# Thresholded attention and a feed-forward on one core: scores of pairs 2 and 3 computed twice, thresholds subtracted by the matrix engine, and a new order of the work

## The chip, the core and the metric

The kernel runs on one core of a Trainium2 chip. The core has a matrix engine (TensorE, PE in the profile; its weight loads are PEld), a vector engine (VectorE, DVE), a scalar engine for activation functions (ScalarE, ACT), a general engine (GpSimd, POOL) and an engine that here only issues transfers (SyncE, SP). Each runs its own list of instructions; they wait for each other through semaphores. Data lie in the main memory (DRAM), in the on-chip memory of 128 partitions, or in PSUM, the memory that PE writes its sums to. The metric is the device time of one execution in microseconds (us), as the median of several runs.

## The reference

Attention over 8 batches with 8 heads of 576 positions and 64 features, in which only scores near the maximum of their row count; then a feed-forward of two matrix products over the 4608 positions with 512 features:

```python
scores = scale * np.matmul(q, k.transpose(0, 1, 3, 2))
thresh = np.max(scores, axis=-1, keepdims=True) - tau
scores = np.where(scores >= thresh, scores, -1000000000.0)
scores = scores - np.max(scores, axis=-1, keepdims=True)
attn = np.exp(scores)
attn = attn / (np.sum(attn, axis=-1, keepdims=True) + 1e-09)
out = np.matmul(attn, v)
# x: the heads side by side, (4608, 512)
h = x @ w_in                              # 512 -> 2048
g = h * (1.0 / (1.0 + np.exp(-1.702 * h)))
return g @ w_out                          # 2048 -> 512
```

tau is 0.02. The weights arrive as 64-bit floats.

## The kernel before

**Pairs of heads.** The 64 heads are worked on as 32 pairs, n = 0 to 31, four to a batch. For a pair, q and k are loaded (`load_qk`, four DMAs each on SP's queue) and transposed by DVE (`prep`, L477). PE computes the scores with the keys in the partitions, one key tile j of 64 keys at a time, nine tiles in all (`scores`, L493: four matmuls of 64x288 for two heads and two halves of the queries). ACT copies each from PSUM (`keep`, L510). DVE takes the maxima over groups of keys (`in_groups`, L516, with a transpose in the instruction), then over tiles (`over_tiles`, L525) and over the halves of the keys (`over_halves`, L536 to L547), where the gap tau/scale is also subtracted. The thresholds, one for each query, must then be spread over all partitions. For pairs in `BY_DMA` they go through a row in DRAM: `turn_rows` (L553), `row_out` (L566) and `row_in` (L575), on SP's queue. Pair 2 alone uses a DVE transpose instead (`spread_max`, L557). Then, for double key tiles t, DVE subtracts the thresholds from the scores (`sub`, L580), ACT drives what is negative to a huge negative number (`mask`, L586) and takes the exponential (`exps`, L590), and PE multiplies by the values (`values`, L601).

**Denominators.** For pairs 0 to 4 PE sums the exponentials with a matrix of ones (`sums_by_pe`, L601) and DVE reads the sums (`one_row`, L632). For the others DVE sums in groups. For pairs 5 to 7 the sums are folded and spread by DVE (`one_group`, L643 to L647, `spread_sums`, L684 to L686); from pair 8 on they go through a row in DRAM (`turn_sums`, `sums_out`, `sums_in`). `place_x` (L703) multiplies the values by the reciprocals and places the pair in the input of the feed-forward.

**Feed-forward.** It runs in blocks of 256 positions. The first two blocks go together and need pairs 0 to 3 (`mm1_0`, L758, then ACT's tanh, L727, and DVE's `gelu_0`, L764, then `mm2`, L740). The third block needs pairs 4 to 7, and so on. From the third block on (first products at L718) the second product takes seven block products in place of eight, and the last four blocks do so for the first one too (L823, L909). The weights come in 32 pieces of 1 MB on POOL's queue (`load_w`, L428 and L429). DVE and ACT turn each into 32-bit floats (L439, L453, L457, L465 on DVE, L447 on ACT). The places where the pieces land are free again only after a piece before them is done.

**The order.** Nothing is scheduled by hand. Each step is recorded as a task with an engine, a cost, a rank, the tasks that it comes after, and the buffers that it takes and gives back. `run_in_order` then plays the tasks through with these costs, and writes each engine's list in the order in which they start. A rank is the number of the pair plus a bias by the step's name, from the tables `EARLY` (pairs 0 to 3), `SECOND` (4 to 7), `LATER` and `CV` (weights). The lists are fixed afterwards: an instruction waits behind the one in front of it on its engine, whatever the chip does.

**Buffers that matter.** `psA` has three PSUM buffers for scores and values, `psM` two for denominators and the feed-forward. A single row buffer serves the thresholds of one pair at a time. The value tau is loaded on POOL's queue at the start; `tau_terms` on DVE needs it.

The lines that choose the pairs:

```python
BY_PE = 5
BY_DMA = (0, 1, *range(3, NP))
SUMS_BY_DMA = range(8, NP)
```

Of the kernel before, what the change touches and what calls it, by code (L numbers as in the profile page):

```python
# [19 lines left out]
P = 128  # L20
# [10 lines left out]
def kernel(  # L31
# [84 lines left out]
    stop = const.tile([P, 1], FP32, name="stop")  # L116
    shift = const.tile([P, 1], FP32, name="shift")
# [9 lines left out]
    for x in ("raw0", "raw1", "qkT0", "qkT1", "mb"):  # L127
# [6 lines left out]
        "exps": -11.47,  # L134
        "in_groups": 5.75,
        "keep": 10.66,
        "load_qk": -0.27,
        "load_v": 4.86,
        "mask": -2.66,
        "one_group": -15.86,  # L140
        "one_row": 12.67,
        "over_halves": -7.01,
        "over_tiles": -4.01,
        "place_x": -17.11,
        "prep": -11.73,
        "row_in": 20.49,
        "row_out": 4.47,
        "scores_run": 12.45,
        "spread_max": -1.73,
        "spread_sums": 7.14,  # L150
        "sub": 9.27,
        "sums_by_pe": 0.27,
        "sums_in": -9.39,
        "sums_out": 2.13,
        "turn_rows": -12.55,
        "turn_sums": -0.41,
        "values": 14.64,
        "w_sum": 4.11,
        "x_sum": -14.1,
    }  # L160
    SECOND = {
        "exps": -7.29,
        "in_groups": 20.95,
        "keep": 16.67,
        "load_qk": -8.88,
        "load_v": 5.53,
        "mask": 2.36,
        "one_group": 2.55,
        "one_row": -2.71,
        "over_halves": -12.07,  # L170
        "over_tiles": 2.86,
        "place_x": -20.26,
        "prep": 3.49,
        "row_in": -19.42,
        "row_out": -24.08,
        "scores_run": -7.99,
        "spread_max": -3.11,
        "spread_sums": -2.29,
        "sub": 14.98,
        "sums_by_pe": 35.93,  # L180
        "sums_in": 7.43,
        "sums_out": 4.05,
        "turn_rows": -3.84,
        "turn_sums": 4.03,
        "values": 11.79,
        "w_sum": -10.45,
        "x_sum": -10.98,
    }
    LATER = {
        "exps": 2.01,  # L190
        "in_groups": 10.37,
        "keep": -0.02,
        "load_qk": -6.6,
        "load_v": 3.77,
        "mask": 14.79,
        "one_group": 4.78,
        "one_row": -14.98,
        "over_halves": 1.09,
        "over_tiles": -6.27,
        "place_x": -0.34,  # L200
        "prep": 2.34,
        "row_in": 4.02,
        "row_out": 2.64,
        "scores_run": -11.25,
        "spread_max": -9.44,
        "spread_sums": -6.73,
        "sub": 2.14,
        "sums_by_pe": 1.46,
        "sums_in": 3.78,
        "sums_out": 2.16,  # L210
        "turn_rows": 12.26,
        "turn_sums": 0.29,
        "values": -10.38,
        "w_sum": 6.61,
        "x_sum": 6.02,
    }
    CV = {
        "cv_end": -8.05,
        "cv_ex": 2.22,
        "cv_frac": -11.72,  # L220
        "cv_power": -4.72,
        "load_w": -7.79,
    }

    LAG = {"PE": 0.26, "DVE": 0.18, "ACT": 0.22, "POOL": 0.18}

    QUARTERS = ("scores", "scores_run", "values", "sums_by_pe")
# [12 lines left out]
    FIRST, LAST = -9.0, 1000.0  # L240
    need, follows = {}, {}

    def run_in_order():
# [12 lines left out]
        while events:  # L256
# [18 lines left out]
            for engine, queue in ready.items():  # L275
                if engine in busy:
                    continue
                for rank, i in sorted(queue):
# [25 lines left out]
    JOINT = 7  # L304

# [183 lines left out]
    def scores(n, j):  # L489
# [8 lines left out]
        if j == NK - 1:  # L498
            del mats[n, 0], mats[n, 1]
# [32 lines left out]
    def over_halves(n):  # L532
        r = stats[n, ALU.max]
        o = work.tile([P, QB], FP32, name="fold", tag="fold", bufs=1)
        for x in (1, 3) if n in BY_DMA else range(4):
            nc.vector.tensor_scalar(  # L536
                out=o[ts(x ^ 1, 32)], in0=r[ts(x, 32)], scalar1=gap[ts(x, 32)], scalar2=None,
                op0=ALU.subtract,
            )
        if n in BY_DMA:  # L540
# [10 lines left out]
    def turn_rows(n):  # L551

        nc.vector.transpose(out=flat[1], in_=flat[0])  # L553

# [23 lines left out]
    def sub(n, t):  # L578
        s = sT[n, t].rearrange("p u h s -> p u (h s)")
        nc.vector.tensor_tensor(  # L580
# [26 lines left out]
    def values(n, tiles):  # L607
# [4 lines left out]
        if n < NPAIR:  # L612
# [763 lines left out]
```

## Time and profile before

| | us |
|---|---|
| median of 3 runs | 1318.74 (1318.22 to 1318.92) |
| the profiled execution, its time | 1317.94 |
| its span, first to last instruction | 1316.2 |
| pair 3 placed (start of L703) | 114.40 |
| last weight piece ready (L465) | 215.3 |
| pair 7 placed (start of L703) | 276.40 |
| first product of the third block (L718) | 280.23 |

The costliest groups on the three busy engines are these (line, engine, operation, output and inputs, count; then busy time and the mean of one in ns; then the idle time ahead of them and what ended it).

```profile
L516 DVE TRANSPOSE_TENSOR_REDUCE part<-arena 128x36 f32<-128x1152 f32 (+1 forms) x295 | 357.5, 1235 | 41.9 <-ACT arena L510 32.4
L718 PE MATMUL hps<-xT,w_in 128*128 128x256 f32 x1536 | 337.2, 380 | 0.5 <-DVE arena L730 0.4
L510 ACT COPY arena<-ps 128x576 f32<-128x576 f32 x288 | 170.7, 647 | 115.3 <-PE ps L493 111.9
L580 DVE TENSOR_TENSOR arena<-arena 128x1152 f32<-128x1152 f32 (+1 forms) x158 | 201.1, 1313 | 20.5 <-DMA arena<-row 20.5
L493 PE MATMUL ps<-arena 64*64 64x288 f32 x2304 | 174.7, 420 | 22.9 <-DVE arena L477 15.3
```

A matmul of 32-bit floats appears as two records, so the 1152 score matmuls of 32 pairs are 2304 records; [...]the mean of 420 ns is not the time between two of them. DVE's subtraction is one of its large groups. PE's idle time ahead of the scores waits mostly for DVE's transposes in the start-up.

### The profile page before, as it was taken

The numbers are of one execution on the slowest core, as the hardware profiler recorded it, in microseconds if no ns is written. First come the engines' busy times: TensorE is split into PE (matmuls) and PEld (weight loads), VectorE is DVE, ScalarE is ACT, GpSimd is POOL, SyncE is SP. The second block draws the span as 40 slices with busy tenths as digits, with TensorE's granted clock in tenths as the row PEclk, the third lists the DMA queues.
The fourth block names the chain that finished last, engine by engine and source line by source line (L and its number), as shares of the span: only waits on it lengthen the run. The fifth ranks groups of instructions, "written<-read, shape, count | busy, mean of one in ns | idle before, by whom it ended". The sixth has DMA issues, their size and how long they took to land. (4 is left out here: it accounts for less than half of the span.)

```text
span 1316.2 us, 22807 instructions
## 1 busy us (share of the span) xinstructions
PE 1260.9 (96%) x9128; PEld 975.6 (74%) x9128; DVE 1006.1 (76%) x1610; ACT 646.6 (49%) x830; POOL 249.0 (19%) x291
## 2 busy tenths in 40 slices
PE   5669999999999999999999999999999999999998
PEld 2346864457887777777778888777777778888887
DVE  7989999898888887788777877777888863652642
ACT  4876666576554555555554555454556540210210
POOL 1201211012031211213021303030212117120120
PEclk8879999999999999999999999999999999999999
DMA  8976766545323223212213222323122110000000
GB/s 152 293 189 207 230 207 149 112 77 100 85 55 71 55 55 71 51 50 54 58 42 72 55 71 55 71 55 71 36 55 54 36 46 8 9 1 25 8 0 32
DMA packets 258819, 102.88 MB, mean 78 GB/s; under 512 B 233754, under 2 KB 243994, under 8 KB 258714
## 3 DMA queue, kind: packets, MB, share of 16 engines
q1 hardware_dynamic: 244986, 63.40, 22.4%
q0 software_dynamic: 11360, 37.74, 9.3%
q8 instruction: 71, 1.16, 0.4%
q10 hardware_dynamic: 2368, 0.30, 0.2%
q14 instruction: 34, 0.28, 0.1%
HBM read 87.51 MB, written 9.69 MB: 74 GB/s over the span
## 5 line engine op out<-in xcount | busy, mean ns | idle before, releaser
L516 DVE TRANSPOSE_TENSOR_REDUCE part<-arena 128x36 f32<-128x1152 f32 (+1 forms) x295 | 357.5, 1235 | 41.9 <-ACT arena L510 32.4
L718 PE MATMUL hps<-xT,w_in 128*128 128x256 f32 x1536 | 337.2, 380 | 0.5 <-DVE arena L730 0.4
L718 PEld LDWEIGHTS hps<-xT,w_in 128*128 128x128 f32 x1536 | 290.7, 190 | 45.9 <-issue 5.7
L586 ACT ACTIVATE arena<-arena 128x1152 f32<-128x1152 f32 (+1 forms) x160 | 169.4, 1059 | 144.0 <-DVE arena L580 143.8
L510 ACT COPY arena<-ps 128x576 f32<-128x576 f32 x288 | 170.7, 647 | 115.3 <-PE ps L493 111.9
L580 DVE TENSOR_TENSOR arena<-arena 128x1152 f32<-128x1152 f32 (+1 forms) x158 | 201.1, 1313 | 20.5 <-DMA arena<-row 20.5
L909 PE MATMUL ops<-w_out,arena 128*128 128x256 f32 x896 | 202.4, 380 | 1.8 <-DVE arena L730 1.8
L590 ACT ACTIVATE arena<-arena,shift,scl 128x1152 f32<-128x1152 f32 (+1 forms) x160 | 200.3, 1252 | 4.1
L493 PE MATMUL ps<-arena 64*64 64x288 f32 x2304 | 174.7, 420 | 22.9 <-DVE arena L477 15.3
L909 PEld LDWEIGHTS ops<-w_out,arena 128*128 128x128 f32 x896 | 169.3, 190 | 28.7 <-DVE arena L730 3.1
L875 POOL TENSOR_TENSOR arena<-arena 128x256 f32<-128x256 f32 x56 | 49.7, 888 | 647.1 <-DVE arena L730 543.9
L601 PE MATMUL pv<-arena 64*64 64x288 f32 x2176 | 159.7, 408 | 0.0
L727 ACT ACTIVATE th<-hps 128x512 f32<-128x512 f32 x112 | 66.0, 589 | 186.0 <-PE hps L718 171.8
L909 PE MATMUL ops<-arena 128*128 128x256 f32 x672 | 150.7, 380 | 0.7 <-DVE osb L931 0.7
L493 PEld LDWEIGHTS ps<-arena 64*64 64x64 f32 x2304 | 84.0, 137 | 90.8 <-ACT arena L510 30.4
L909 PEld LDWEIGHTS ops<-arena 128*128 128x128 f32 x672 | 127.1, 190 | 20.4 <-issue 2.2
L601 PEld LDWEIGHTS pv<-arena 64*64 64x64 f32 x2176 | 82.1, 134 | 54.1 <-issue 10.0
L931 DVE SCALAR_TENSOR_TENSOR osb<-ops,osb 128x256 f32<-128x256 f32 x98 | 39.3, 413 | 97.9 <-PE ops L909 90.6
L730 DVE SCALAR_TENSOR_TENSOR arena<-th,hps 128x512 f32<-128x512 f32 x96 | 64.2, 669 | 46.7 <-ACT th L727 46.4
L740 PE MATMUL ops<-w_out,arena 128*128 128x512 f32 x128 | 57.2, 600 | 3.2 <-DVE w_out L465 2.2
L758 PE MATMUL hps<-xT,w_in 128*128 128x256 f32 x256 | 56.4, 381 | 0.0
L888 POOL TENSOR_TENSOR arena<-arena 128x512 f32<-128x512 f32 x28 | 35.6, 1272 | 108.3 <-PE ops L909 108.3
(115 smaller groups left out, 1044.7 us busy)
## 6 DMA issues: line engine op xcount, KB each, us to landing
arena<-in_v_dram SPq DMA_DIRECT2D x128, 144.0 KB
arena<-in_q_dram SPq DMA_DIRECT2D x128, 72.0 KB
out_dram<-osb SPq DMA_DIRECT2D x36, 256.0 KB
arena<-in_k_dram SPq DMA_DIRECT2D x124, 72.0 KB
arena<-row SPq DMA_DIRECT2D x62, 144.0 KB
arena<-row_s SPq DMA_DIRECT2D x48, 144.0 KB
w_out<-in_moe_w_in_dram POOLq DMA_DIRECT2D x12, 512.0 KB, 9.5
arena<-in_moe_w_out_dram POOLq DMA_DIRECT2D x12, 512.0 KB, 6.3
```

The costliest lines, as they stand in the source:

```text
L493: nc.tensor.matmul(ps[ts(c, KT), h, 0:SH], lhsT=mats[n, 1][ts(h, D), ts(j, KT)], rhs=mats[n, 0][ts(h, D), ts(c, SH)], start=True, stop=True,)
L510: nc.scalar.copy(out=sT[n, t][:, u], in_=pss.pop((n, j))[:, :, 0:SH])
L516: nc.vector.tensor_reduce(out=stats[n, op][:, t * 2 * QB : min(2 * t + 2, NK) * QB], in_=sT[n, t].rearrange("p u h (g d) -> p (u h g) d", ...
L580: nc.vector.tensor_tensor(out=s, in0=s, in1=mbs[n].unsqueeze(1).to_broadcast(list(s.shape)), op=ALU.subtract)
L586: nc.scalar.activation(out=s, in_=s, func=AF.Prelu, alpha=STEEP)
L590: nc.scalar.activation(out=s, in_=s, func=AF.Exp, scale=scl, bias=shift)
L601: nc.tensor.matmul(o[c][ts(h, D), 0:SH], lhsT=left(j, h)[ts(c, KT)], rhs=sT[n, t][ts(c, KT), u, h, :], start=(j == 0), stop=(j == NK - 1),)
L718: nc.tensor.matmul(hidden[j][:, ts(f, BLK)], lhsT=w_in[:, c, ds((f * HF + j) * P, P)], rhs=xTs[blk][:, c, :], start=(c == 0), stop=(c == N ...
L727: nc.scalar.activation(out=ths[j], in_=hidden[j], func=AF.Tanh, scale=GELU_SCALE / 2)
L730: nc.vector.scalar_tensor_tensor(out=g[:, :, j, :], in0=two(ths.pop(j)), scalar=1.0, in1=two(hidden.pop(j)), op0=ALU.add, op1=ALU.mult,)
L740: nc.tensor.matmul(acc[i], lhsT=g0[:, j, ts(i, P)], rhs=w_out[:, j, :], start=(j == 0), stop=(j == NFC - 1),)
L909: nc.tensor.matmul(banks[blk][k][:, ts(o, HM)], lhsT=left[:, j, :], rhs=right[:, j, :], start=(j == 0), stop=(j == HF - 1),)
```

## The change

It has four parts.

1. **Pairs 2 and 3 (`TWICE`).** DVE no longer subtracts. The thresholds are laid out on DVE as a matrix that has, in each partition, only the queries of one group (`row_blocks`: a small transpose and a product with `own_row`, a matrix of ones and zeros). When the maxima are known, PE computes each score tile again (`again`), and adds to the same PSUM sum the product of this matrix with `minus`, which holds -1 and 0. ACT masks straight out of PSUM (`mask_one`, nine for a pair) into the place where the copied scores lay. Pair 3 no longer sends its thresholds through DRAM, and pair 2 no longer uses `spread_max`. `minus` and `own_row` are set up once on POOL, in front of tau's load.
2. **Sums of pairs 5 to 7** go through a row in DRAM, as those of pairs 8 and later do.
3. **The planner** has two more servers, DMS and DMW, for transfers from SP's and POOL's queues. A load is now a task for the issue and a task for the transfer, with a cost, one at a time on each server and in the order of arrival. Some costs of tasks are new. `BY_POOL`, which would move subtractions to POOL, is empty.
4. **All ranks** (`EARLY`, `SECOND`, `LATER`, `CV`, `W_RANK`) are new.

```diff
+    minus = const.tile([P, 2, KT], FP32, name="minus")
+    own_row = const.tile([P, QB // 2], FP32, name="own_row")
...
+    MOVERS = ("DMS", "DMW")
+    def transfer(by, time, a, give=(), lag=1.7):
+        return task(by, time, FIRST, moved, after=[a], give=give, lag=lag)
...
-                for rank, i in sorted(queue):
+                for rank, i in queue if engine in MOVERS else sorted(queue):
...
+    TWICE = (2, 3)
+    BY_POOL = {}
...
+        if n in TWICE:
+            for x, y in ((0, 0), (1, 2), (2, 1), (3, 3)):
+                nc.vector.scalar_tensor_tensor(
+                    out=flat[0][ts(y, 32), 0:QB], in0=r[ts(x, 32)], scalar=gap[ts(x, 32)],
+                    in1=o[ts(x, 32)], op0=ALU.subtract, op1=ALU.max,
+                )
+            return
...
+    def row_blocks(n):
+        nc.vector.transpose(out=flat[1], in_=flat[0])
+        mb = home(n, "mb")[:, 0:SH]
+        nc.vector.tensor_tensor(
+            out=mb.rearrange("p (g i) -> p g i", i=32),
+            in0=flat[1].unsqueeze(1).to_broadcast([P, QB // 2, 32]),
+            in1=own_row.unsqueeze(2).to_broadcast([P, QB // 2, 32]), op=ALU.mult,
+        )
+        mbs[n] = mb
+
+    def again(n, j):
+        ps = psA.tile([P, 2, 512], FP32, name="ps", tag="ps")
+        for first in (True, False):
+            for h in range(2):
+                for c in range(2):
+                    if first:
+                        left = mats[n, 1][ts(h, D), ts(j, KT)]
+                        right = mats[n, 0][ts(h, D), ts(c, SH)]
+                    else:
+                        left, right = minus[ts(h, D), c, :], mbs[n][ts(h, D), :]
+                    nc.tensor.matmul(
+                        ps[ts(c, KT), h, 0:SH], lhsT=left, rhs=right, start=first, stop=not first,
+                    )
...
+    def mask_one(n, j):
+        nc.scalar.activation(
+            out=sT[n, j // 2][:, j % 2], in_=pss.pop((n, j))[:, :, 0:SH], func=AF.Prelu, alpha=STEEP
+        )
...
+    nc.gpsimd.memset(minus, 0.0)
+    nc.gpsimd.memset(own_row, 0.0)
+    for x in range(4):
+        nc.gpsimd.memset(minus[ts(x, 32), x % 2, :], -1.0)
+        nc.gpsimd.affine_select(
+            out=own_row[ts(x, 32)], in_=own_row[ts(x, 32)], compare_op=ALU.not_equal, fill=1.0,
+            base=-(QB // 2) * (x // 2), pattern=[[-1, QB // 2]], channel_multiplier=1,
+        )
     nc.gpsimd.dma_start(
         out=tau_b, in_=bass.AP(tensor=tau.tensor, offset=tau.offset, ap=[[0, P], [1, 1]])
     )
...
-    BY_PE = 5
-    BY_DMA = (0, 1, *range(3, NP))
-    SUMS_BY_DMA = range(8, NP)
+    SUMS_BY_PE = (0, 1, 2, 3, 4)
+    BY_DMA = (0, 1, *range(4, NP))
+    SUMS_BY_DMA = range(5, NP)
...
-        a = task("POOL", 1.1, rank, load_w, i, after=w_loads[-1:], take=place, lag=9.0)
+        a = task("POOL", 1.1, rank, load_w, i, after=w_loads[-1:], take=place)
         w_loads.append(a)
-        e = task("DVE", 0.345, rank, cv_ex, i, after=[a])
+        a = transfer("DMW", 4.0, a)
+        e = task("DVE", 0.42, rank, cv_ex, i, after=[a])
...
+            if n in TWICE:
+                for j in range(2 * t, min(2 * t + 2, NK)):
+                    m = task(
+                        "PE", 0.97 * slow, r, again, n, j, after=[m], take=("psA",),
+                        give=own(n, "qkT0", "qkT1", "mb") if j == NK - 1 else (),
+                    )
+                    a = task("ACT", 0.62, r, mask_one, n, j, after=[m] + mx, give=("psA",))
+                ws.append(task("ACT", 0.76 if tail else 1.24, r, exps, n, t, after=[a]))
+                continue
```

## The prediction

> Pairs are counted from 0 as in the code, so the third and fourth are pairs 2 and 3. "Changed order" means the order in which each engine's instructions stand in the changed program, which is known without a run.
>
> **What bounds the kernel now.** First the page: busy time of each engine, and the slices.
>
> ```profile
> PE 1260.9 (96%) x9128; PEld 975.6 (74%) x9128; DVE 1006.1 (76%) x1610; ACT 646.6 (49%) x830; POOL 249.0 (19%) x291
> PE   5669999999999999999999999999999999999998
> PEclk8879999999999999999999999999999999999999
> ```
>
> TensorE (PE) works 96% of the span; its idle time, 1316.2 - 1260.9 = 55.3 us, is all there is to win, and it stands in the first slices. Second, stretches of the first 140 us (columns: length, busy time of each engine with its count, granted clock, DMA share, GB/s).
>
> ```profile
> 0.00:20.00 20.00, 11.57 (x144) 5.03 (x144) 11.65 (x22) 10.93 (x20) 1.25 (x9) 1.00 0.91 135
> 20.00:40.00 20.00, 7.07 (x76) 3.94 (x80) 19.54 (x27) 9.28 (x14) 6.87 (x14) 0.73 0.86 249
> 40.00:60.00 20.00, 15.64 (x214) 8.71 (x211) 19.66 (x35) 19.41 (x19) 3.20 (x6) 0.92 1.04 326
> 60.00:80.00 20.00, 10.05 (x152) 4.82 (x144) 18.78 (x29) 15.45 (x21) 4.23 (x8) 0.84 0.87 248
> 80.00:100.00 20.00, 17.19 (x220) 13.08 (x224) 15.85 (x32) 15.39 (x15) 0.00 (x0) 0.81 0.58 100
> 100.00:120.00 20.00, 17.48 (x227) 9.74 (x222) 18.06 (x39) 16.70 (x27) 3.18 (x6) 0.91 0.61 189
> 120.00:140.00 20.00, 20.00 (x97) 17.48 (x93) 19.38 (x31) 6.27 (x10) 4.47 (x8) 1.00 0.60 195
> ```
>
> PE is idle 41.0 us up to 120 us and then full. VectorE (DVE) is nearly full until about 277 us, where pair 7 is placed (277.2) and the third block of the feed-forward starts (280.2). By stretches of ten, PE idles 6.4 us between 120 and 280 and 7.8 us after that, 3.4 of them after 1200. Third, the waits between 60 and 125 us, and in the timelines the ends of the start-up (PE, ACT) and the use of GpSimd (POOL).
>
> ```profile
> PE den L601 <- DVE r L632: 10.8, 1, 10.8
> DVE arena L580 <- DMA arena<-row: 3.7, 1, 3.7
> ```
> ```profile
> 117.60 1.99 PE L758 MATMUL hps<-xT,w_in 128*128 128x256 f32 x8
> 120.17 39.98 PE L758 MATMUL hps<-xT,w_in 128*128 128x256 f32 x184
> ```
> ```profile
> 36.13 1.16 ACT L586 ACTIVATE arena<-arena 128x1152 f32<-128x1152 f32 x1 [3.46 <-DVE arena L580]
> 100.42 0.87 ACT L590 ACTIVATE arena<-arena,shift,scl 128x576 f32<-128x576 f32 x1
> ```
> ```profile
> 1.39 0.75 POOL L948 DMA_DIRECT2D tau_b<-in_tau_dram  x1 [0.35 <-issue]
> 290.10 0.73 POOL L875 TENSOR_TENSOR arena<-arena 128x256 f32<-128x256 f32 x1 [5.36 <-DVE arena L730]
> ```
>
> PE waits 10.8 us for sums of pair 1 that DVE reads late, DVE 3.7 us for pair 3's thresholds from DRAM. Four feed-forward matmuls (1.74 us) go ahead of 120.17, so the feed-forward starts in effect at 118.4. What counts is that time and PE's idle time after it.
>
> **What the Trainium skill says.** "PSUM — Partial Sum Buffer", Engine vs sequencer instructions: the queues of ScalarE, VectorE and GpSimdE are strictly in order. The trace agrees: pair 1's sums were finished on PE at 61.9, but their read stood in DVE's queue until 80.95. "GPSIMD Engine Reference", 2.1 Instruction dispatch: the first call into a freshly loaded library pays a code load of about 6 us. Both programs have one library reload on POOL: before, ahead of the first TENSOR_TENSOR shown; changed, ahead of the first affine_select, in front of tau's load. POOL's previous work ended at 284.74 and that TENSOR_TENSOR started at 290.10, 0.1 us after DVE's release: the trace shows at most 5.3 us, not 6, and no lower end. "TensorE: Matmul & The Clock Gate", Part 1: after an idle window of about 3.4 us the clock falls. The trace has 0.73 at 20 to 40 us with PE idle for 13 us; the extra matmuls could hold it up there, and I give them no gain for it.
>
> **The change, part by part.**
>
> *Scores twice.* PE: 18 key tiles x 8 matmuls. Eight matmuls of this form take 0.97 us (sixteen records, two for each fp32 matmul, between one group at 203.61 and the next at 204.58), so 17.5 us of new PE work, all before the feed-forward. The 41 us of idle time cover it; without that cover it would cost all 17.5. DVE: away are 8 subtractions of 1.27 us and 2 of 0.67 (-11.5). New are, net, 2 small subtractions and 6 small maxima at 0.26 and a small transpose of 0.14 (+2.2), 2 products of 128x288 at about 0.5 each (nearest row: 128x256 at 0.42, +1.0), less pair 2's 0.70 transpose and 0.27 maximum. Sum: -9.3 us. Pair 3 also loses its trip through DRAM, 77.78 to 88.56 in the timeline. ACT: 18 masks out of PSUM at 0.65 (as the 128x576 copy, 0.647) for 8 of 1.155 and 2 of 0.67: +1.1 us.
>
> *Where the saving goes.* Summed by row over the changed order, DVE's work up to pair 3's placement is 100.8 us against 101.5: pair 4's maxima (6.3 us) now stand in front of it, with one weight piece more. The relief appears only after it: 145.0 against 155.7 us until pair 7 is placed. So the start-up depends on ACT. From ACT's first mask to pair 3's last exponential the trace has 65.2 us, of which 9.1 idle: 56.0 of work. The changed order has +1.1 for masks, eight copies of pair 4 (x 0.62 = 5.0) and two weight powers (1.4) before that exponential: 63.5 us. Its first mask comes later, since a weight piece (1.41 + 0.64) and pair 1's thresholds (1.2) stand before DVE's first subtraction, and pair 1's transposes between pair 0's maxima: 39.2 by adding durations from 6.79 on. Idle is left where PE's first repeated tile is awaited (1.6) and between tiles (about 2). 39.2 + 63.5 + 3.6 = 106.3, against 101.3.
>
> *From there to the feed-forward.* PE then has the last denominators (0.5), 28 value matmuls of pair 2 (3.4), 36 of pair 3 (4.4) and 12 scores (1.5), with half a microsecond of denominators still queued: 116.7. DVE has pair 4's thresholds in front of the placement: 119.5, where before has 115.3. The 28 last scores of pair 5 run at the pace of ACT's copies, between which two weight powers wait for DVE: feed-forward at 122.5, **+4.1 us** on 118.4.
>
> *Tau.* New memsets and four affine_selects (nearest rows 0.10 to 0.18) put the load at about 3.5 us plus the reload; it lands 3.9 later, as before. DVE wants it at 8.2, and behind the waiting instruction stand pair 0's maxima and pair 1's transposes, for which PE's scores and ACT's copies wait in turn. Reload 0: lands at 7.4, cost 0. Reload 5.3: lands at 12.7, DVE 4.5 late, of which 2.2 remain, since its first maximum waited for ACT until 11.22 anyway. I take a reload near 4 us: **+1.5** (0 to 2.2). No gain is possible, as nothing got earlier.
>
> *After the start.* PE has 155.4 us of work from there to the third block (160.1 + 1.7 less 6.4 idle), the same in both. DVE ends its 16 w_out pieces after 79 us of work instead of 98, so about 199 instead of 214.6: PE's waits for them (0.6 and 1.6, and the 0.9 of a late copy) go. What is late next is the first second-layer matmul on its last activation (0.95 in before), since DVE has 70 us of work from pair 3's placement to the sixteenth activation, and PE gets there 69 us after it starts. I keep 3.1 of 6.4 us idle: **-3.3** (-6 to 0).
>
> *Sums of pairs 5 to 7 through DRAM.* A DVE saving of three 0.84 transposes and about 0.4 per pair, contained in the 145.0. The two DMA pairs on SP's queue stand before later row and q/k loads; the nearest trip, 10.8 us for pair 3 under load, has PE's feed-forward as cover, and only past pair 7's placement at about 270 would it be paid. Taken 0, at most +2.
>
> *New ranks in later pairs, transfers modelled.* The matmul work is the same; the order on DVE, ACT and SP is new, and 4.4 us of idle time stood there before the final 3.4. It can win 2 and lose 5 or more, as each pair's miss stalls PE alone: **+1**. The transfer model only sets the order: a first weight piece landed 8.1 us after its issue (26.01, 34.16).
>
> Sum: +4.1 + 1.5 - 3.3 + 1.0 = +3.3. The profiled execution (1317.94: span 1316.2 and 1.7 around it) would become 1321.2; on the median, 1318.74, 0.8 higher, **1322.0**.
>
> **The rivals.** Within 0.2% (2.6 us) is called no change, about what these runs can tell apart.
> - *A, forecast: ACT and the later placement keep the feed-forward back.* For it: the ACT sum; against: about 3 us of idle time in a walk are easily misjudged. 1322, own range 1318.5 to 1327.
> - *B, faster: PE's start.* If the copies of pairs 4 and 5 fall into ACT's gaps and placement is at 113, the feed-forward starts at about 116, and with the later -3.3 stands at -5 to -6: 1313. For it: pair 3's 10.8 us trip and PE's 10.8 us wait are gone. It decides from a start below about 117.
> - *C, no change: DVE's relief pays back the late start exactly*, reload hidden, 1319.
> - *D, clearly slower: the new ranks stall PE in the later pairs*, at a third of a microsecond for each of 24 pairs, about +8 over A: 1330. For it: DVE is 78 to 86% busy there; against: PE was full from 500 to 1000 us.
> - *The subtraction in PSUM doesn't take work off the limit:* it moves the limit to ACT and is part of A.
>
> **How the numbers follow.** A 0.40, B 0.23, C 0.15, D 0.22. Two thirds of A are over the bound, the rest within. Faster: B, 0.23. Slower: 0.22 from D and 0.26 from A, 0.48. Same: 0.15 and 0.14, 0.29. The range of 8 in 10 reaches into B and D, leaving out a third of B and half of D: 1311.5 to 1331.
>
> **What would show it.** A first feed-forward matmul near 124 with ACT without gaps from 40 to 106 confirms A; a start below 117, B. The wait of DVE's first small operation on tau's load shows the reload; PE's waits on L465's counterpart near 200 to 215 gone, the middle part. PE idle over 8 us past 300 would be D. Wrong would be the forecast if PE, not ACT, paced the repeated tiles: it needs 1.94 us for two, ACT 2.6.

## The result and the profile after

The changed kernel takes 1336.83 us in the median (1333.9 to 1337.4, four runs), against 1318.83 for the kernel before in the same session: a ratio of 1.0127 (95% interval 1.0104 to 1.0149). It is slower. The prediction was 1322.0 with a range to 1331; the direction came true, the size did not. The profiled execution took 1336.89, with a span of 1335.1.

The page of the changed kernel, busy times and slices:

```profile
PE 1278.8 (96%) x9416; PEld 988.3 (74%) x9416; DVE 990.5 (74%) x1600; ACT 647.7 (49%) x838; POOL 248.1 (19%) x301
PE   5599799899999999999999999999999999999998
PEclk8799899999999999999999999999999999999999
```

PE has 17.9 us more work than before (17.5 were counted for the repeated scores), and its idle time is 1335.1 - 1278.8 = 56.3 us, against 55.3. Taken over the whole run, the added work was not hidden: up to the first matmul of the feed-forward PE's idle time fell from 41.0 to 32.6 us, and about as much idle time came up elsewhere. In the PE line the fifth digit (134 to 167 us) and the eighth (234 to 267) are no longer full. Where the time went is seen from two milestones, the first matmul of the feed-forward and the first product of its third block:

| us | before | after | difference |
|---|---|---|---|
| start, up to the first feed-forward matmul | 117.60 | 123.94 | +6.3 |
| middle, from there to the third block (PE idle in it) | 162.63 (6.4) | 167.26 (10.5) | +4.6 |
| the rest (PE idle in it) | 1035.97 (7.8) | 1043.90 (13.2) | +7.9 |

The prediction counted 118.4 for the start of before, since 1.74 us of matmuls go ahead there. By its count the differences are +5.5, +5.4 and +7.9, where it had +5.6 (4.1 and 1.5), -3.3 and +1.0.

The stretches of the changed kernel that answer to those of before (length, busy time of PE, PEld, DVE, ACT, POOL with counts, granted clock, DMA share, GB/s):

```profile
20.00:40.00 20.00, 6.07 (x68) 3.02 (x64) 18.14 (x25) 7.24 (x13) 7.33 (x15) 0.75 0.79 245
60.00:80.00 20.00, 19.00 (x275) 14.30 (x271) 17.90 (x42) 15.28 (x23) 1.07 (x2) 0.90 0.55 106
120.00:140.00 20.00, 13.70 (x96) 10.30 (x88) 11.34 (x20) 12.26 (x17) 3.18 (x6) 0.98 0.87 235
140.00:160.00 20.00, 18.40 (x100) 15.09 (x104) 18.43 (x31) 11.72 (x15) 4.32 (x8) 0.85 0.48 165
```

From 60 to 80 us PE is now nearly full, where it worked 10.05 of 20 us before: there the repeated tiles found their room. From 120 to 140, where PE was full before, it works 13.70, and DVE only 11.34 of 20. The table of waits of the whole run names both sides (engine and tile, what it waited for; total, times, longest; the other wait of the first line is for the first load of all):

```profile
DVE arena L498 <- DMA arena<-in_q_dram: 15.5, 2, 8.6
PE hps L820 <- DVE arena L826: 7.0, 1, 7.0
PE ps L514 <- ACT arena L531: 5.8, 3, 3.5
PE hps L780 <- DVE arena L792: 5.6, 8, 1.4
```

L498 is the transpose of q and k (`prep`), L826 the first blocks' gelu, L531 the copy of the scores, L792 the later gelu. The timeline of the changed kernel shows how the first two lines hang together (start, length, engine, line; in brackets the idle time before it and what ended it):

```profile
125.73 2.50 SPq L387 DMA_DIRECT2D arena<-in_q_dram  x4
126.74 0.53 POOL L449 DMA_DIRECT2D w_out<-in_moe_w_out_dram  x1 [13.17 <-DVE w_in L486]
...
128.28 11.19 SPq L387 DMA_DIRECT2D arena<-in_k_dram  x4
128.33 0.69 DVE L826 SCALAR_TENSOR_TENSOR arena<-th,hps 128x512 f32<-128x512 f32 x1
128.94 2.62 DVE L642 TENSOR_TENSOR arena<-arena 128x1152 f32<-128x1152 f32 x2
...
140.19 0.78 DVE L498 STREAM_TRANSPOSE arena<-arena 128x576 f32<-128x576 f32 x1 [8.64 <-DMA arena<-in_q_dram]
140.90 0.65 DVE L826 SCALAR_TENSOR_TENSOR arena<-th,hps 128x512 f32<-128x512 f32 x1
...
141.60 0.80 PE L820 MATMUL hps<-xT,w_in 128*128 128x256 f32 x1 [7.03 <-DVE arena L826]
```

SP issues pair 6's q at 125.73. One microsecond later POOL starts to issue six transfers of half a megabyte, three pieces of `w_out`. DVE is ready for the transpose of q at 131.55 and stands still for 8.64 us. Behind it in DVE's list stands a gelu which needs nothing from that load, and PE's next product waits for this gelu. In the kernel before, the loads of pair 6 were issued at 134 to 140 and wanted only at 155.66, without a wait:

```profile
134.49 3.42 SPq L366 DMA_DIRECT2D arena<-in_q_dram  x4
155.66 1.43 DVE L477 STREAM_TRANSPOSE arena<-arena 128x576 f32<-128x576 f32 x2
```

So q had 21 us from its issue to its use, and has 6 us now. The Trainium skill, "DMA: Bandwidth & Descriptors", Issuing engines are not separate DMA queues, says that transfers from SP and POOL run on the same 16 DMA engines and interleave. The trace agrees: the DMA share was 1.04 from 134 to 138 us at 386 GB/s, and q could be used 14.5 us after its issue. Which load comes late differs: in a second profile of the changed kernel DVE waited 0.71 us for q and 5.76 for k, up to 142.13, and PE 5.46 behind it. That the pieces of `w_out` delay these loads is read from the DMA share; no run took them away. The changed planner has two servers, one for each queue, that don't share time, and lets a load of q cost 3.2 us and a lag of 1.7.

The stall costs more than its length. Stretches of 2 us around its end, in the changed kernel:

```profile
130.00:132.00 2.00, 2.00 (x11) 1.77 (x10) 1.56 (x2) 1.68 (x3) 0.00 (x0) 1.00 1.10 301
136.00:138.00 2.00, 0.00 (x0) 0.00 (x0) 0.00 (x0) 0.12 (x1) 0.00 (x0) 1.00 1.06 382
142.00:144.00 2.00, 2.00 (x6) 1.56 (x6) 1.97 (x4) 0.82 (x2) 0.00 (x0) 0.50 0.04 8
144.00:146.00 2.00, 2.00 (x6) 1.58 (x5) 2.00 (x5) 1.97 (x2) 0.00 (x0) 0.50 0.00 0
148.00:150.00 2.00, 2.00 (x11) 1.76 (x10) 2.00 (x4) 1.94 (x3) 0.00 (x0) 1.00 0.86 348
```

After the wait the granted clock is 0.50, and PE gets through 6 matmul records in 2 us in place of 11. Over the 4 us from 142 to 146 that is 10 records of 0.18 us short, 1.8 us, so that the wait and the slow matmuls come to about 8.8 us in this execution. The middle was predicted 8.7 us too short.

### The profile page after: what moved, and what is told of

It is laid out like the page before. It is cut to its first block, busy times and chain, and to the rows that moved or that the text cites. A ratio compares the mean times of both kernels' runs of the same rounds, so it can differ in the third digit from the quotient of the medians.

```text
span 1335.1 us, 23381 instructions
## 1 busy us (share of the span) xinstructions
PE 1278.8 (96%) x9416; PEld 988.3 (74%) x9416; DVE 990.5 (74%) x1600; ACT 647.7 (49%) x838; POOL 248.1 (19%) x301
## 3 DMA queue, kind: packets, MB, share of 16 engines
q8 instruction: 74, 1.21, 0.4%
## 4 chain that ended last, share of the span: by engine, by line
PE 67%; DVE 12%; DMA 8%; ACT 7%; SPq 3%; issue 2%; DVEq 0%; POOL 0%; ACTq 0%
PE ops L971 22%; PE hps L780 16%; PE pv L663 8%; PE ps L514 8%; PE ps L885 4%; PE ps L971 4%; DVE part L537 3%; ACT arena L652 3%; PE ops L885 3%; DMA arena<-row 3%; DVE arena L642 3%; ACT arena L648 2%; DMA arena<-in_k_dram 2%; DMA arena<-in_q_dram 1%; PE hps L820 1%
## 5 line engine op out<-in xcount | busy, mean ns | idle before, releaser
L780 PE MATMUL hps<-xT,w_in 128*128 128x256 f32 x1536 | 339.8, 381 | 5.9 <-DVE arena L792 5.6
L780 PEld LDWEIGHTS hps<-xT,w_in 128*128 128x128 f32 x1536 | 289.8, 190 | 54.8 <-DVE arena L792 10.7
L648 ACT ACTIVATE arena<-arena 128x1152 f32<-128x1152 f32 (+1 forms) x150 | 158.5, 1057 | 164.7 <-DVE arena L642 164.7
L531 ACT COPY arena<-ps 128x576 f32<-128x576 f32 x288 | 170.3, 645 | 140.4 <-PE ps L514 140.4
L642 DVE TENSOR_TENSOR arena<-arena 128x1152 f32<-128x1152 f32 (+1 forms) x149 | 188.4, 1306 | 37.7 <-DMA arena<-row 37.7
L792 DVE SCALAR_TENSOR_TENSOR arena<-th,hps 128x512 f32<-128x512 f32 x96 | 63.9, 665 | 38.6 <-ACT th L789 36.9
L820 PE MATMUL hps<-xT,w_in 128*128 128x256 f32 x256 | 59.1, 392 | 7.0 <-DVE arena L826 7.0
L820 PEld LDWEIGHTS hps<-xT,w_in 128*128 128x128 f32 x256 | 49.7, 196 | 16.6 <-DVE arena L826 7.9
L498 DVE STREAM_TRANSPOSE arena<-arena 128x576 f32<-128x576 f32 x64 | 45.8, 744 | 20.5 <-DMA arena<-in_q_dram 15.5
```

What stands on the lines that cost most here:

```text
L531: nc.scalar.copy(out=sT[n, t][:, u], in_=pss.pop((n, j))[:, :, 0:SH])
L642: engine.tensor_tensor(out=s, in0=s, in1=mbs[n].unsqueeze(1).to_broadcast(list(s.shape)), op=ALU.subtract)
L648: nc.scalar.activation(out=s, in_=s, func=AF.Prelu, alpha=STEEP)
L780: nc.tensor.matmul(hidden[j][:, ts(f, BLK)], lhsT=w_in[:, c, ds((f * HF + j) * P, P)], rhs=xTs[blk][:, c, :], start=(c == 0), stop=(c == N ...
L820: nc.tensor.matmul(hidden[j][:, ts(i, BLK)], lhsT=w_in[:, c, ts(j, P)], rhs=xTs[i][:, c, :], start=(c == 0), stop=(c == NDC - 1),)
```

## The experiments

All runs of one group were compared with runs of the kernel before on the same chip, at 1317.0 to 1318.2 us in the median. Ratios are to these. First a table of the milestones, in us, with the stretches of the table above; it is referred to below. The time is the median of all executions, while the stretches are those of the one that was profiled, and this one can lie some us off the median: it took 1335.70 us where the median is 1330.45 (delays 0.04 less), 1335.58 where it is 1338.98 (score products left out) and 1326.84 where it is 1331.02 (first version for pairs 8 and 11). The start varies too: in five profiles of the changed kernel in which nothing is altered up to there, it lies between 123.1 and 125.9.

| run | time | ratio (95%) | start | middle | rest |
|---|---|---|---|---|---|
| before (first profile) | 1318.83 | 1 | 117.6 | 162.6 | 1036.0 |
| changed, again | 1335.96 | 1.0140 (1.0125 to 1.0155) | 124.0 | 166.4 | 1043.5 |
| lag of pair 6 in the plan | 1333.24 | 1.0098 (1.0067 to 1.0129) | 125.8 | 158.9 | 1047.8 |
| lag of all pairs from 5 | 1333.73 | 1.0104 (1.0074 to 1.0134) | 123.8 | 163.8 | 1043.3 |
| pair 6's transposes moved by hand | 1329.56 | 1.0093 (1.0073 to 1.0113) | 125.9 | 158.6 | 1043.7 |
| and k of pairs 8 and 11, first version | 1331.02 | 1.0093 (1.0071 to 1.0114) | 123.1 | 158.6 | 1043.3 |
| and k of pairs 8 and 11, second version | 1328.61 | 1.0086 (1.0071 to 1.0101) | 125.2 | 159.0 | 1043.3 |
| score products of `again` left out | 1338.98 | 1.0155 (1.0136 to 1.0175) | 124.4 | 165.6 | 1043.7 |
| ranks `LATER` of before | 1333.54 | 1.0123 (1.0105 to 1.0141) | 125.3 | 164.9 | 1041.3 |
| these and pair 6 by hand | 1326.94 | 1.0059 (1.0041 to 1.0077) | 123.9 | 160.3 | 1042.0 |
| one server for transfers | 1351.81 | 1.0256 (1.0232 to 1.0281) | 149.4 | 162.3 | 1039.2 |
| all ranks of before in the changed kernel | 1350.15 | 1.0226 (1.0191 to 1.0261) | 139.0 | 168.2 | 1042.1 |
| before + sums by rows | 1332.03 | 1.0095 (1.0062 to 1.0128) | 117.2 | 169.8 | 1043.5 |
| before + scores twice | 1333.59 | 1.0121 (1.0097 to 1.0145) | 125.4 | 168.5 | 1037.0 |
| before, delays 0.04 more | 1325.46 | 1.0067 (1.0050 to 1.0084) | 116.9 | 169.4 | 1035.0 |
| before, delays 0.04 less | 1330.45 | 1.0087 (1.0054 to 1.0119) | 118.0 | 169.4 | 1046.5 |
| before, other costs of pieces | 1344.96 | 1.0188 (1.0151 to 1.0224) | 122.9 | 170.6 | 1048.5 |
| before, three steps moved by hand | 1317.54 | 0.9993 (0.9982 to 1.0005) | 116.3 | 157.8 | 1040.3 |

The first theory was that the planner's belief in early arrivals puts transposes ahead of their loads; its rivals were the new ranks, the repeated work itself and the sums by rows.

**The lag in the plan.** One number of the planner, for pair 6 alone and then for all pairs from 5 on (8.0 there):

```diff
-        lq, lk = (transfer("DMS", 3.2, a) for a in (lq, lk))
+        late = 14.0 if n == 6 else 1.7
+        lq, lk = (transfer("DMS", 3.2, a, lag=late) for a in (lq, lk))
```

> The changed kernel with one number of the planner altered: the transfers of q and k of pair 6 count as landed 14.0 us after their server is done, instead of 1.7. Theory 1 (the planner believes in an arrival that the w_out pieces on the DMA engines make impossible, so that the transposes of pair 6 stand ahead of the gelu on VectorE): VectorE's wait of 8.64 us and TensorE's of 7.03 us near 134 to 141 us go, the first product of the third block moves from 291.2 to 284 to 287, the time falls from 1336.8 to 1330 to 1333. Rival (the wait only shows where VectorE's backlog is taken; the 18.9 us lost lie in the work and order after it): the third block still starts near 291, the time stays at 1336.8 within 1.5.

> The changed kernel with the transfers of q and k of all pairs from 5 on counted as landed 8.0 us after their server is done, instead of 1.7. Theory 1 extended (early belief in arrivals also makes the stalls at 255 and at 311 to 325 us, together about 7 us of TensorE's idle time): below the single-pair version, at 1325 to 1330, with less than 9 us idle of TensorE past 291. Rival (these stalls come from the new ranks, which order maxima, subtractions and gelus): the same as the single-pair version within 2 us, 1330 to 1334.

The stall at 134 to 141 us goes in both, and the middle falls by 8.3 us for pair 6. But the time falls by only 3 to 4, for pair 6 to just above the range expected and for all pairs no further, as the rival had it. The plan becomes another one and stalls elsewhere: for pair 6 PE waits 3.94 us for a gelu at 316. For all pairs the waits from 311 to 325 shrink, and a PE wait of 5.63 us at 254 takes their place. With a planner between the edit and the order, an edit is not one edit. So the next runs kept the order.

**The same by hand.** The planner's order is recorded, single steps are moved in it, and then it is issued. Only DVE's list changes:

```diff
-                tasks[i][3](*tasks[i][4])
+                order.append(i)
...
+        (('prep', 6, 0), ('cv_end', 18)),
+        (('prep', 6, 1), ('prep', 6, 0)),
```

> The changed kernel with its order of work kept, except that VectorE's two transposes of pair 6 (q and k) stand some twelve instructions later, behind the eighteenth weight piece, where their loads have landed by the first trace. Theory 1 (a transpose ahead of its load holds up everything behind it): VectorE's wait of 8.64 us and TensorE's of 7.03 us go, the first product of the third block moves from 291.2 to 284 to 286, time 1329 to 1332. Rival (the backlog only passes to the next wait, or the time is lost again later): third block later than 288, time 1335 or above.

As expected: the span falls from 1335.1 to 1328.2, the median from 1336 to 1329.6, and the third block starts at 284.5. In the timeline of this version, PE in the first fence and DVE in the second, no wait is left there:

```profile
125.90 24.44 PE L833 MATMUL hps<-xT,w_in 128*128 128x256 f32 x112
150.27 4.59 PE L676 MATMUL pv<-arena 64*64 64x288 f32 x72
```

```profile
146.64 1.42 DVE L511 STREAM_TRANSPOSE arena<-arena 128x576 f32<-128x576 f32 x2
```

PE runs 24 us without a break where it had stood for 7, and the two transposes follow each other with no wait at all. The middle is 158.6 us, and 158.6 and 159.0 in the two versions that follow: 2.8 to 3.2 less than the 161.8 that the prediction started from (280.23 - 118.4), where it had -3.3. Without this one stall the length that it gave the middle holds. What is in it differs a little: PE works 154.5 us where 155.4 were counted, and stands idle 4.1 where 3.1 were kept, all in one wait for a copy on ACT:

```profile
248.45 1.53 PE L527 MATMUL ps<-arena 64*64 64x288 f32 x16 [4.11 <-ACT arena L544]
```

The run as a whole gains less than the 8.8 us of the stall: 6.2 us by the ratios (1.0140 to 1.0093), or 4.5 from the first measurement of the changed kernel (1.0127). One reason is in the profiles: here the feed-forward starts 2.0 us later than in the first profile, as DVE waited 1.64 us for pair 5's k. With the stall such a delay is hidden: in four profiles that have it the third block starts at 290.1 to 291.2, whether the start is at 123.9 or at 125.3.

**The later transposes.** Two moves more, k of pair 8 and of pair 11. In a first version they were moved past the load that reuses the buffer, so that it works with wrong keys for pairs 8 and 11. In the second they stay in front of that load.

> As the run with the transposes of pair 6 moved, and also VectorE's transposes of k of pairs 8 and 11 behind the sums of pair 6 and a gelu. Theory 1 for the later stalls: TensorE's wait of 3.50 us at 255 and part of the 3.1 us between 311 and 325 go, 3 to 6 us below the run with pair 6 alone: 1324 to 1328. Rival (these waits come from VectorE's load of work under the new ranks, the transposes only show it): within 1.5 us of the run with pair 6 alone.

> The changed kernel with its order kept, except that VectorE's transposes of q and k of pair 6 stand some twelve instructions later, k of pair 8 two later and k of pair 11 five later, where their loads should have landed; the output is the reference's. Theory 1 for the later stalls: TensorE's waits near 250 (4.1 us with pair 6 alone moved) and some of those between 306 and 320 (2.9 us) go, 3 to 6 us below the run with pair 6 alone, 1324 to 1327. Rival (they come from VectorE's load under the new order; the transposes only show it): within 1.5 us of it, 1328 to 1331.

1328.61 against 1329.56: the time is the rival's. PE's wait near 250 went from 4.11 to 3.23 us, those at 306 to 321 stayed (0.72 and 2.02, against 0.71, 1.53 and 0.66). But the reason is not quite the rival's, that DVE is loaded with work. Its two waits for k are gone (1.95 us at 231 and 3.23 at 312 with pair 6 alone), and in their place it waits longer for rows of thresholds, 2.17 us at 236 and 3.08 at 318, against 1.00 and 0.31. The next load in its list is late as well.

**The repeated products.** The score matmuls of `again` are left out, so the output is that of thresholds alone; the order is kept.

```diff
-        for first in (True, False):
+        for first in (False,):
```

> The changed kernel with its order of work kept, and without the repeated score products of pairs 2 and 3: only the product that subtracts the thresholds is left in the repeated tiles, 8.7 us of TensorE's work less (the output is another). Theory 2 (ScalarE's and VectorE's chain sets the start of the feed-forward, as predicted): first feed-forward matmul within 1.5 us of 123.9, time 1335 to 1338. Rival (TensorE's repeated work delays the start): first feed-forward matmul at 117 to 121, time 1329 to 1333.

The first feed-forward matmul stands at 124.44, with 7.3 us less PE work ahead of it (84.04 busy, against 91.38), and the time, 1338.98, is no lower; it lies a little above the range expected. So the repeated score products are not what sets the start, as predicted, or by little: ACT's last exponential of pair 3 ended at 106.61 there, 1.6 us sooner than in the changed kernel, but then DVE waited 2.14 us for pair 5's k. The product that subtracts was still in. That ACT's chain sets the start is read from timelines, and no run tests it. In the changed kernel its first mask and its last exponential of pair 3 stand at

```profile
39.37 1.16 ACT L648 ACTIVATE arena<-arena 128x1152 f32<-128x1152 f32 x1 [3.74 <-DVE arena L642]
107.39 0.87 ACT L652 ACTIVATE arena<-arena,shift,scl 128x576 f32<-128x576 f32 x1
```

where 39.2 was predicted for the mask, and 106.3 for the end of the exponential (108.26 in the trace). The sum is right to 2 us, but its two terms are not: between these points ACT works 60.2 us, where 63.5 were counted, and stands idle for 8.7, where 3.6 were. It waited 2.28 us at 52.97, because DVE had waited 6.42 us for pair 1's thresholds, whose way through DRAM fell beside weight pieces (DMA share 1.05 from 44 to 48 us), and 3.06 and 1.01 us at 71 and 73 for PE's scores.

**Ranks.** The table `LATER` of before in the changed kernel, all tables of before in it, and `LATER` together with the two moves by hand:

> The changed kernel with the table of ranks of the pairs from 8 on taken from before (the new steps get the ranks of those that they replace); the start and the stall at 134 to 141 stay. Theory 3 (the new ranks of later pairs cost the extra idle time past the third block, 13.2 against 7.8 us): 1330 to 1333, idle time past the third block under 9 us. Rival (that idle time comes from the transfers' costs and from the backlog of the first 290 us): 1335 or above, or idle past the third block over 11 us.

> The changed kernel with the ranks of before (the three steps that are new take the ranks of the steps that they replace). Theory of ranks (the new ranks cost the 7.9 us after the start of the third block): 1326 to 1331, with TensorE's idle time past the third block's start at 8 us or less. Rival (ranks are not what is at fault; the transfer model and the repeated scores are): 1335 or above, and a stall on a load of q or k again between 125 and 290.

> The changed kernel with both edits that gained: the ranks of pairs from 8 on as before, and VectorE's transposes of pair 6 some twelve instructions later in the order so planned. If the two losses are apart (the stall at 134 to 141 us, and the order of the later pairs), their gains add: 7 and 2.5 us off 1336, 1325 to 1328, idle time of TensorE past the third block near 10 us, none over 2 us between 125 and 200. If they are one backlog: no better than with pair 6 alone, 1329 or above.

With `LATER` of before the rest takes 1041.3 us, with 10.0 idle, and with both edits 1042.0, with 10.8 idle. In six profiles with the new table it takes 1043.3 to 1043.9. So some 2 of the 7.9 us belong to that table, less than the theory had, though the time, 1333.54 against 1335.96, is barely apart. Both edits add up, to 1326.94, as two separate losses would. The ranks of before as a whole don't fit the new tasks: 1350.15, with the start at 139 and a wait of DVE for a load of k again (4.23 us at 151.88), as the rival had it.

**Parts of the change alone.** The kernel before with `SUMS_BY_DMA = range(5, NP)`, and with the scores of pairs 2 and 3 twice:

> The kernel before with the sums of pairs 5 to 7 through a row in DRAM, nothing else (its planner and ranks unchanged). Prediction's term: 0, at most +2: 1317.5 to 1320.8. Rival (the trips of these sums delay the placement of pair 7 or stand in front of loads on SP's queue): +3 or more, above 1322, with the third block later than 280.2.

> The kernel before, with its planner and ranks, and the scores of pairs 2 and 3 twice with the thresholds subtracted in PSUM as the only part of the change. The prediction's terms for this part (+4.1 at the start, -3.3 after it): 1317 to 1323, feed-forward at 119 to 124. Rival (any new set of tasks under ranks not made for it gives new stalls, as the sums by rows alone did, at 1332): 1327 or above, with a TensorE wait of over 5 us after the start.

Each part alone, under the planner and the ranks of before, costs nearly as much as the whole change, as both rivals had it: 0.95% and 1.21%, or 12.5 and 16 us by the ratios. For the sums by rows a part of this can be seen. DVE waits 4.50 us for a row of sums at 252.50, behind that ACT's masks wait 9.93, and PE 8.04 at 270.84, where it waited 2.16 in before:

```profile
252.50 0.95 DVE L703 TENSOR_TENSOR xT<-pv,arena 128x192 f32<-128x192 f32 x4 [4.50 <-DMA arena<-row_s]
```

The changed kernel has no wait of DVE for a row of sums between 120 and 340 us. So the two runs can't simply be added up: either the parts are each bad and hide each other, or something costs in every new plan. The next runs ask that.

**A new plan without content.** The kernel before, with the planner's delays 0.04 us longer, then 0.04 shorter, and with other costs for the steps of a weight piece. The work of every engine is the same; only the order is planned anew.

```diff
-    LAG = {"PE": 0.26, "DVE": 0.18, "ACT": 0.22, "POOL": 0.18}
+    LAG = {"PE": 0.3, "DVE": 0.22, "ACT": 0.22, "POOL": 0.18}
```

> The kernel before with the planner's delays after TensorE's and VectorE's instructions at 0.30 and 0.22 us instead of 0.26 and 0.18, nothing else: the work is the same, the order is planned anew with no aim. Theory 4 (a large share of the loss is that of any new order: the order of before has few transposes, reads and subtractions in front of late transfers, and a new plan does not keep that): 1323 to 1333. Rival (an order planned with nearly the same costs is as good; the loss belongs to the parts of the change): 1317 to 1321.

> The kernel before with the planner's delays after TensorE's and VectorE's instructions at 0.22 and 0.14 us instead of 0.26 and 0.18, nothing else. Theory 4 (any order planned anew loses several us, in whichever direction the numbers are moved): 1321 to 1333. Rival (the larger delays made a worse plan; smaller ones needn't): 1314 to 1320.

> The kernel before with the changed kernel's costs for the three VectorE tasks of a weight piece (0.42, 1.14, 0.70 for 0.345, 1.1, 0.61), nothing else: a part of the change that the prediction gave no cost. Theory 4: 1321 to 1333. Rival (costs nearer to the trace, where the four instructions of a piece take 0.39, 0.42, 0.69 and 0.69 us, make a better order): 1318 or below.

+9, +11 and +25 us by the ratios, for numbers that change nothing in the chip's work. The third set is nearer to the trace than the old one, and does worst. The middle is 6.7 to 8.0 us longer in all three; the rest goes from -1.0 to +12.5. The places are much the same as after the change: PE waits near 250 in all three, and near 315 to 325 in two. In the timeline of the version with shorter delays, DVE and then PE:

```profile
235.27 0.78 DVE L477 STREAM_TRANSPOSE arena<-arena 128x576 f32<-128x576 f32 x1 [3.85 <-DMA arena<-in_k_dram]
314.62 1.36 DVE L580 TENSOR_TENSOR arena<-arena 128x1152 f32<-128x1152 f32 x1 [6.94 <-DMA arena<-row]
```

```profile
246.78 2.20 PE L493 MATMUL ps<-arena 64*64 64x288 f32 x16 [3.78 <-ACT arena L510]
316.63 16.50 PE L718 MATMUL hps<-xT,w_in 128*128 128x256 f32 x64 [5.56 <-DVE arena L730]
```

DVE stands at a load, ACT's copies or the gelus stand behind it, and PE behind those. The order of before has few such places on the chip, and these changes of numbers gave that up: between 120 and 340 us DVE waits 5.5 us for transfers in before, 15.7 after the change, and 7.0, 16.1 and 19.0 with the three sets of numbers. It is not shown that the whole loss of the changed kernel has this reason: its plan comes from ranks of its own, not from those of before with other numbers.

**One server.** The weight pieces on the same server as the loads of the pairs:

```diff
-        a = transfer("DMW", 4.0, a)
+        a = transfer("DMS", 4.0, a)
```

> The changed kernel with one server for all transfers in the planner instead of two, so that a weight piece and the loads of a pair no longer cost time side by side; nothing else. If the two servers are what puts pair 6's transposes too early: no TensorE wait of over 3 us between 130 and 150, 1327 to 1333. Rival (the plan is new again, and makes stalls elsewhere of the size that plans of before made with other numbers, 8 to 26 us above before): 1327 to 1343 with waits of 3 us or more near 250 or 315.

Now the start is the loss: PE waits 15.71 us for a threshold matrix up to 74 and 5.40 for the other up to 125, the feed-forward begins at 149.4, and 6.37 us more are lost up to 266. 1351.81 lies above every range that was expected. A model nearer to the shared DMA engines in one point gave a worse plan; whether the two servers as such place pair 6's transposes too early stays open.

**The cause put to use in before.** In the order of before, ACT's first mask and exponential of pair 8 are put behind three copies of scores, and the last weight piece is finished ahead of the placement of pair 5:

```diff
+        (('mask', 8, 0), ('keep', 9, 6)),
+        (('exps', 8, 0), ('mask', 8, 0)),
+        (('place_x', 5), ('cv_end', 31)),
```

> The kernel before with its order kept, except that ScalarE's first mask and exponential of pair 8 stand behind three more copies of scores out of PSUM, and the last weight piece's final step stands ahead of the placement of pair 5 on VectorE. By the cause found (what stands in front in a list holds up what TensorE waits for) TensorE's waits of 2.16 us at 271 and of 1.63 us at 215 shrink by some 2 and 0.9: 1314.5 to 1316.5. Rival (the waits only pass to the next product): 1317 to 1318.5.

No difference that can be measured, as the rival had it. The wait of 2.16 us at 271 is gone, and the third block starts at 274.08 in place of 280.23; then PE waits for the first gelu, which stands behind six maxima on DVE that were not moved (the timeline of DVE, then of PE):

```profile
276.44 7.63 DVE L530 TRANSPOSE_TENSOR_REDUCE part<-arena 128x36 f32<-128x1152 f32 x6
284.00 0.64 DVE L744 SCALAR_TENSOR_TENSOR arena<-th,hps 128x512 f32<-128x512 f32 x1
```

```profile
284.69 2.57 PE L732 MATMUL hps<-xT,w_in 128*128 128x256 f32 x8 [3.02 <-DVE arena L744]
```

What PE gained, it gave back at the next thing that DVE owes it. No version here is faster than the kernel before.

## Why the prediction was wrong

- **The start: right, in part by luck.** 122.5 and 1.5 for tau were predicted, 124.0 together; the trace has 123.94. ACT's first mask held, and the repeated score products were not the limit, or by 1.6 us at most. But tau's 1.5 did not come, and ACT's chain ended 2.0 us later than predicted, with less work (60.2 for 63.5 us) and more waiting (8.7 for 3.6). The sign that was named, ACT without gaps from 40 to 106, did not show. What was missing was the wait for pair 1's row.
- **Tau: wrong, at 1.5 for 0.** GpSimd's first affine_select starts 0.06 us after the memset in front of it ended, and tau's load is issued at 2.90; DVE reads tau at 8.2 without a wait. This is the case "Reload 0" of the prediction. The four selects take 0.19 us each. Of the code load of some 6 us for which the prediction named the Trainium skill's "GPSIMD Engine Reference", 2.1 Instruction dispatch, nothing is seen here.
- **The middle: the step that failed.** "I keep 3.1 of 6.4 us idle: -3.3". The waits for the pieces of `w_out` did go, and DVE was relieved: both are in the run with pair 6 moved, where the middle is 3.2 us shorter. But the step asked only which waits would go and which of the old ones would be next. It had the changed order on DVE, and did not lay the new places of the transposes against the time at which their loads can land. Pair 6's q was now wanted about 24 us sooner than before, beside three weight pieces. That cost 7.0 us of waiting and 1.8 of low clock in the profiled execution, and the middle took 5.4 us more in place of 3.3 less; moving the two transposes alone took 4.5 to 6.2 us off the median.
- **"The transfer model only sets the order": true, and the order is what costs.** How much of it is the model's and how much the ranks', the runs don't tell. The model was given nothing, and the new ranks +1 with "win 2 and lose 5 or more". The rest took 7.9 us more: 5.4 of it PE's idle time, 2.5 longer matmul records, with the same 7089 of them. Some 2 of the 7.9 are shown to belong to the table `LATER`. For the others no single cause is shown; plans without any new content had from -1.0 to +12.5 there.
- **Sums by rows: open.** 0 to 2 was predicted. Alone they cost 12.5 us, with a wait of their own, 4.50 us for a row of sums, which the changed kernel doesn't have. But it was a new plan, and new plans alone cost 9 to 25, so that the runs can't tell their own part.
- **The rivals.** D, stalls in the later pairs, came true by its own mark (13.2 us idle past 300), and its 1330 was the nearest figure. But the largest single loss was of D's kind in A's place, in the second group of pairs, where nobody was looking. B fell at the start, as it was said it would.

## What to carry to other kernels

When a change passes through a planner, price the new plan itself: nudge a number without meaning in the old kernel and see what that costs, before anything is put down to the parts of the change. Then take each load in the new order, from its issue to the instruction that needs it, and ask what else the DMA engines carry in between and what stands behind that instruction in its list. A wait that is taken away by moving one step is a gain only as far as the next thing that the same busy engine owes.

## What was not expected of the hardware

PE's wait of 7.0 us was followed by a granted clock of 0.50 up to about 146 us, some 4.5 us after work began again at 141.6, which adds a quarter to its price. The Trainium skill, "TensorE: Matmul & The Clock Gate", Part 1, has the clock at half after an idle window of about 3.4 us and full again after a busy one of the same length; the trace agrees in kind, with a little more on the way back. The prediction drew on it for the start alone and put no clock into the price of a stall. Four loads of 72 KB (pair 6's q) could be used only 14.5 us after their issue beside three pieces of 1 MB; in the second profile q could be used after 7.1 us, and k after 14.6.
